# First two pairs of heads rearranged, and odd heads' score tiles in other units

## Chip, cores and metric

One core of one Trainium2 chip. The metric is device microseconds of a whole execution, as the median of several runs. TensorE does matmuls and transpositions, VectorE, ScalarE and GpSimd (POOL) work on tiles, SyncE (SP) issues most transfers; ScalarE can issue transfers too.

## What is computed

Attention that keeps only keys close to the row's largest score, then two feed-forward blocks. All in float32, results to float32 accuracy.

```python
# q, k, v: (4, 8, 576, 64); tau = 0.02
scores = q @ k.T / sqrt(64)
keep   = scores >= max(scores, -1) - tau
attn   = where(keep, exp(scores - max), 0);  attn /= sum(attn) + 1e-9
x      = (attn @ v) as rows of 2304 tokens x 512
h      = x @ w_in                       # 512 x 2048
x      = where(h >= 1, h, where(h <= -1, 0, (h + 1)**2 / 4)) @ w_out
h      = x @ w_in2                      # 512 x 1024
s      = h * softmax(h);  x = layernorm(s) * g_ln
out    = x @ w_out2
```

## The kernel before

Each float32 factor is held as a high part in the matmul's own format and a low part, the rounding rest, so a product of two factors takes several matmuls. For scores, the high and low parts of k and of q are stacked along the contraction: `k_st` and `q_st` hold 128 rows, `k_on` and `q_m` up to 67, of which three serve the row shifts. The stacking moves data between partitions and is done by transfers.

There are 32 heads in 16 pairs. A head has 5 score tiles of 128 queries by 576 keys. **Score tiles** (`sc`, `scores`) are only needed for the row maxima (`mcol`, `row_max`, VectorE). `row_shift` turns a head's five maxima into shifts (two ScalarE steps, three POOL steps), `shift_turn` transposes them on TensorE, `shift_store` copies them on ScalarE and sends them into `q_m` from ScalarE's queue. After that the **shifted tiles** (`zt`, `shifted`) are computed transposed, with the keys on partitions; `expo` (ScalarE) and `mask` (VectorE) follow, `p_split` makes `phi` (ScalarE) and `plo` (POOL), and three units later `values` does the `av` matmuls.

The unit of the attention loop is one shifted tile. A pair p has the nine units 9p to 9p+8: four tiles of the even head, one tile for the leftovers of both heads (unit 4 of the pair, with eight matmuls in place of four), four of the odd head. Units before 0 only prepare; the loop starts at `U0`. `ORDER` has a string per unit of a pair that says in which order the pieces of a unit are issued: E shifted tile and exp, S a score tile, x a maximum, M mask, v and V value matmuls, p the split, F the split of q and k (`split_kq`: high part `q_st` on ScalarE, low part `lo` on VectorE), P transpositions on TensorE, T transfers and other late things, A ScalarE steps, J one step of the weight jobs. `S_UNITS` says, relative to unit 9p, in which unit each of the ten score tiles of pair p is computed: five of the even head, five of the odd. `T_A` and `T_B` do the same for the transpositions of q and k (`tr`), `at` files a piece under its unit.

`tr`, `sc` and `zt` take turns in three PSUM slots (`ps_r`, three buffers in rotation): an allocation waits for the readers of the one that stood three before it. For `tr` the last reader is VectorE's `lo`, for `sc` the maximum, for `zt` the mask.

The weight jobs decode the first block's first weights, one 128 x 512 piece in many steps on ScalarE, VectorE and POOL. `DECODE` says which kinds of step may run in which unit of a pair (a: arrival, s and b: two kinds of VectorE steps), `JOBS_FROM` from which unit on, a new piece starts every 14 steps.

Each engine runs its instructions in the order written. SP's queue holds the loads of q and k (`load_kq`), of v (`load_v`), of weights and the stacking transfers of `stack_k` and `stack_q`.

Of the kernel before, what the change touches and what calls it, by code (L numbers as in the profile page):

```python
# [21 lines left out]
def kernel(  # L22
# [152 lines left out]
    def setup_fill(first):  # L175

        for i in range(max(NBUF)):
            for j in range(2):
                if i >= NBUF[j] or (i == 0) != first:
                    continue  # L180
# [1 line left out]
                nc.gpsimd.memset(f32(k_st[j][i][:, pad]), 0.0)
                nc.gpsimd.memset(f32(k_on[j][i][:, pad]), 0.0)
                nc.gpsimd.memset(f32(k_on[j][i][D:R3, 64 * j : 64 * j + S]), 1.0)
                nc.gpsimd.memset(f32(k_on[j][i][D:R1, 64 * j : 64 * j + S]), 0.0)
                nc.gpsimd.memset(f32(q_st[j][i][:, S:SP]), 0.0)
                nc.gpsimd.memset(f32(q_m[j][i][0:D, S:SP]), 0.0)
                nc.gpsimd.memset(f32(q_m[j][i][D:R3, :]), 0.0)
        for t in v_nat if first else ():
# [22 lines left out]
    def load_kq(p):  # L212
        t = early_p.tile([P, 2, NM + 1, 2, D], F32, tag="nat", name="nat", bufs=2)
        r0 = 2 * p * S
        two = q_rows[r0 : r0 + 2 * S, :].rearrange("(j s) d -> j s d", j=2)
        for j in range(2):
            nc.sync.dma_start(
                t[:, j, 0:NM, 1, :], two[j, 0:M4, :].rearrange("(p t) d -> p t d", t=NM)
            )
        nc.sync.dma_start(t[0:64, :, NM, 1, :], two[:, M4:S, :].rearrange("j s d -> s j d"))  # L220
# [2 lines left out]
        nc.sync.dma_start(t[:, 0, 0:NM, 0, :], k0)
        nc.sync.dma_start(t[64:P, 1, 0:NM, 0, :], k1[0:64])
        nc.sync.dma_start(t[0:64, 1, 1 : NM + 1, 0, :], k1[64:P])
        for j in range(2):
            nc.sync.dma_start(t[0:64, j, NM * (1 - j), 0, :], k_rows[r0 + M4 + 64 * j : r0 + M4 + 64 * j + 64, :])
        for j in range(2):
            nat_t[2 * p + j] = t[:, j]

    def load_v(p):
# [42 lines left out]
    def stack_k(h):  # L274
        j, i = buf(h)
        kh = f32(q_st[j][i][0:D, 0:S])
        o = slice(key_off(h), key_off(h) + S)
        if h < FAST:
            nc.scalar.copy(k_on[j][i][0:D, o], kh)
            nc.scalar.copy(q_m[j][i][0:D, 0:S], f32(q_st[j][i][D:P, 0:S]))  # L280
            nc.sync.dma_start(f32(k_st[j][i][0:D, o]), f32(k_on[j][i][0:D, o]))
        else:
            nc.sync.dma_start(f32(k_both[j][i][0:D, :, o]), kh.unsqueeze(1).to_broadcast([D, 2, S]))
# [843 lines left out]
```

## Time and profile before

| | us |
|---|---|
| median of 3 runs (984.61 to 988.9) | 985.89 |
| the profiled execution | 985.73 |
| its span, first to last instruction | 983.9 |
| TensorE busy | 953.3 (97%) |
| VectorE, ScalarE, POOL busy | 711.5, 494.6, 603.0 |
| first score tile starts | 18.28 |
| first shifted tile starts | 29.60 |
| first matmul of the feed-forward blocks | 375.89 |

A busy TensorE is not one at its peak: matmuls overlap in the pipeline, and at the lower clock they are busy for longer. Windows give the busy time of each engine in a stretch, with the number of its instructions; the timeline merges instructions of a kind that follow each other, and its bracket tells how long the engine idled before and what ended that; a wait of weight loads (PEld) for something is one of the matmul behind it.

### The profile page before, as it was taken

To read this page: it belongs to the slowest core of one execution; us is meant where nothing else is said; L and a number is where in the kernel's file an instruction comes from. 1 tells how busy PE (TensorE), PEld (TensorE's weight loads), DVE (VectorE), ACT (ScalarE), POOL (GpSimd) and SP (SyncE) were. 2 spreads that over 40 slices of the span, in tenths; PEclk is the share of its full clock that TensorE was granted. 3 is DMA by queue.
4 is the path that set the end of the run, shared out by engine and by line. 5 is a ranking of instruction groups with operands and counts; after the bars stand their busy time and mean duration, and the time that the engine had idled before them with its cause. 6 is when DMAs were issued, how large, how long until landed. Compare 5 with 4: busy or idle time off the path is not lost.

```text
span 983.9 us, 15050 instructions
## 1 busy us (share of the span) xinstructions
PE 953.3 (97%) x5232; PEld 839.6 (85%) x5232; DVE 711.5 (72%) x1128; ACT 494.6 (50%) x926; POOL 603.0 (61%) x573
## 2 busy tenths in 40 slices
PE   4999999999999999999999999999999999999998
PEld 3899988998899988889988998899889988888886
DVE  2788788878778755788767886788775686666561
ACT  2576776776676676454333333333334434434433
POOL 6477877987898788668545643564457704433422
PEclk9999999999999999999999999999999999999999
DMA  6565566666655513221221222111301214434453
GB/s 159 123 138 142 122 134 168 143 164 157 150 137 125 126 50 73 64 77 65 76 74 54 65 65 75 65 65 65 118 31 48 61 43 122 136 108 128 109 143 92
DMA packets 89885, 99.89 MB, mean 102 GB/s; under 512 B 50032, under 2 KB 62640, under 8 KB 89808
## 3 DMA queue, kind: packets, MB, share of 16 engines
...
q10 hardware_dynamic: 384, 0.16, 0.1%
...
## 4 chain that ended last, share of the span: by engine, by line
PE 77%; DVE 7%; ACT 5%; issue 3%; POOL 2%; SPq 2%; DMA 2%; ACTq 1%; DVEq 0%; POOLq 0%
PE y L801 20%; PE h L763 19%; PE o L956 10%; PE h L845 10%; PE av L430 7%; PE zt L380 6%; PE sc L303 4%; DVE e L398 3%; ACT e L393 2%; DVE mcol L316 2%; ACT phi L406 1%; DVE lo L269 1%; PE tr L260 1%; ACT xs L442 1%; DVE raw L501 1%
## 5 line engine op out<-in xcount | busy, mean ns | idle before, releaser
L407 POOL TENSOR_TENSOR plo<-e,phi 128x576 fp32r<-128x576 f32 x144 | 206.6, 1444 | 54.2 <-ACT phi L406 53.7
L784 POOL TENSOR_TENSOR gl<-cl,gh 128x512 fp32r<-128x512 f32 (+1 forms) x80 | 100.4, 1255 | 167.9 <-ACT gh L783 91.7
L801 PE MATMUL y<-gh,wg 128*128 128x512 f32 (+1 forms) x640 | 186.8, 373 | 0.0
L763 PE MATMUL h<-xh,wg 128*128 128x512 f32 (+1 forms) x640 | 184.2, 369 | 0.7 <-DVE e L398 0.7
L398 DVE SCALAR_TENSOR_TENSOR e<-zt,ntau,e 128x576 f32<-128x576 f32 x144 | 117.0, 813 | 63.5 <-ACT e L393 47.3
L801 PEld LDWEIGHTS y<-gh,wg 128*128 128x128 f32 x640 | 118.8, 188 | 17.1
L763 PEld LDWEIGHTS h<-xh,wg 128*128 128x128 f32 x640 | 118.4, 188 | 17.4 <-DVE e L398 1.0
L393 ACT ACTIVATE e<-zt 128x576 f32<-128x576 f32 x144 | 93.6, 650 | 74.7 <-PE zt L380 52.1
L801 PE MATMUL y<-gl,wg 128*128 128x512 f32 (+1 forms) x320 | 120.1, 375 | 0.5 <-POOL gl L784 0.4
L316 DVE TENSOR_REDUCE mcol<-sc 128x1 f32<-128x576 f32 x160 | 117.2, 748 | 3.8 <-PE sc L303 3.6
L763 PE MATMUL h<-xl,wg 128*128 128x512 f32 (+1 forms) x320 | 118.0, 369 | 0.0
L780 ACT ACTIVATE cl<-cl,half 128x512 f32<-128x512 f32 (+1 forms) x80 | 54.4, 680 | 98.5 <-DVE cl L779 98.4
L783 ACT CAST gh<-cl 128x512 fp32r<-128x512 f32 (+1 forms) x80 | 46.3, 578 | 112.5 <-DVE cl L782 106.7
L956 PE MATMUL o<-wg,ln 128*128 128x512 f32 x432 | 102.4, 393 | 0.0
L845 PE MATMUL h<-wg,y 128*128 128x512 f32 x432 | 101.2, 390 | 0.0
L406 ACT CAST phi<-e 128x576 fp32r<-128x576 f32 x144 | 96.3, 669 | 1.5 <-DVE e L398 0.9
L956 PEld LDWEIGHTS o<-wg,ln 128*128 128x128 f32 x432 | 80.9, 188 | 18.4 <-ACT ln L919 0.2
L845 PEld LDWEIGHTS h<-wg,y 128*128 128x128 f32 x432 | 81.0, 188 | 16.8
L920 POOL TENSOR_TENSOR ln<-land,ln 128x1024 fp32r<-128x1024 f32 x16 | 38.5, 2405 | 92.4 <-ACT ln L919 92.4
L779 DVE TENSOR_SCALAR cl<-h 128x512 f32<-128x512 f32 (+1 forms) x80 | 50.6, 632 | 55.1 <-PE h L763 51.3
L380 PE MATMUL zt<-q_st,k_both 128*128 128x288 f32 x320 | 75.1, 316 | 5.1 <-DVE lo L269 3.8
L303 PE MATMUL sc<-k_both,q_st 128*128 128x288 f32 x320 | 72.7, 310 | 5.4 <-DMA q_st<-lo 3.9
...
## 6 DMA issues: line engine op xcount, KB each, us to landing
...
```

The lines of the kernel that those rows point to most:

```text
L303: nc.tensor.matmul(ps[:, c, 0:HS], lhsT=st[j][i][r, n * P : n * P + P], rhs=kk[j][i][r, o + c * HS : o + (c + 1) * HS], start=(st is q_st) ...
L316: nc.vector.tensor_reduce(mc[:, n : n + 1], sc_ps.pop((h, n))[:, :, 0:HS], axis=AXES.XY, op=ALU.max, negate=True)
L380: nc.tensor.matmul(ps[:, c, 0:HS], lhsT=st, rhs=mv[:, c * HS : (c + 1) * HS], start=(m == 0), stop=(m == len(todo) - 1),)
L393: nc.scalar.activation(out=e, in_=st_ps[u][:, :, 0:HS], func=ACTF.Exp)
L398: nc.vector.scalar_tensor_tensor(out=e, in0=st_ps.pop(u)[:, :, 0:HS], scalar=ntau[:, 0:1], in1=e, op0=ALU.is_ge, op1=ALU.mult)
L406: nc.scalar.copy(hi, e)
L407: (nc.vector if u - NU in LO_DVE or u < NU - UNITS and u % UNITS in LO_UNITS else nc.gpsimd).tensor_tensor(lo, e, f32(hi), op=ALU.subtract)
L763: nc.tensor.matmul(ps, lhsT=a[:, kk, f], rhs=m[:, kk, :], start=(n == 0 and kk == 0), stop=(n == 2 and kk == KD - 1),)
L784: nc.gpsimd.tensor_tensor(gl, cl, f32(gh), op=ALU.subtract)
L801: nc.tensor.matmul(y_ps[c][d], lhsT=a[:, jj, ds_], rhs=m, start=(jj == 0 and n == 0), stop=(jj == JG - 1 and n == 2),)
L845: nc.tensor.matmul(ps[g], lhsT=a[:, kk, :], rhs=wg_t["in2", g][s][:, kk, :], start=(n < 2), stop=(n >= 6 * KD - 2),)
L956: nc.tensor.matmul(ps, lhsT=a[:, f, :], rhs=wg_t["out2", f // 4][m][:, f % 4, :], start=(n == 0), stop=(n == len(terms) - 1))
```

## The change

The first two pairs get a schedule of their own, and from the third pair on the odd heads' score tiles stand in units 4, 4, 5, 6, 7 of the pair before in place of 4, 5, 6, 6, 7. The preparation starts at unit -10 instead of -18. Loads of the first two pairs are split over SP's and ScalarE's queues, in another order; the first weight job, the values and the third pair's loads are issued later; stacking of heads 0 and 1 (`split_first`) uses copies on ScalarE, VectorE and POOL and two transfers a head. The fills of the padding are split up, and `keep_warm` adds transpositions of the identity matrix on TensorE, whose result nobody reads. `DECODE` lets no b step run in unit 8, and the weight jobs start at unit 1.

```diff
-    U0 = -18
+    U0 = -10
-    S_UNITS = (-10, -9, -7, -7, -6, -5, -4, -3, -3, -2)
+    S_UNITS = (-10, -9, -7, -7, -6, -5, -5, -4, -3, -2)
+    S_FIRST = ((-8, -7, -6, -5, -4, -3, -2, -1, -1, 0), (-8, -8, -7, -6, -6, -5, -4, -3, -3, -2))
+    WARM = (16, 14, 10)
+    KEEP = {-8: 1, -7: 1, -6: 1, -5: 1, -4: 1, -3: 4, -1: 6, 0: 4, 1: 4, 2: 4}
...
-        "EvvvSSSMxxxVLFPATpJ",
+        "EvvSvSSMxxxVLFPATpJ",
...
-        "FEvvvSSSMxxxVLPvATpJ",
+        "FEvvSvSSMxxxVLPvATpJ",
...
-    JOBS_FROM = -1
+    JOBS_FROM = 1
-    DECODE = ('', '', 's', 'asb', '', 's', '', 'as', 'asb')
+    DECODE = ('', '', 's', 'asb', '', 's', '', 'as', 'as')
...
+        for n, (dst, src) in enumerate(todo):
+            (nc.scalar if n in others else nc.sync).dma_start(dst, src)
...
+    def split_first():
+
+        srcs = [tr_t[h] for h in range(2)]
+        for h in range(2):
+            split_kq(h)
+            j, i = buf(h)
+            o = slice(key_off(h), key_off(h) + S)
+            nc.scalar.copy(k_st[j][i][0:D, o], f32(q_st[j][i][0:D, 0:S]))
+            nc.vector.tensor_copy(k_on[j][i][0:D, o], srcs[h][0:D])
+            nc.sync.dma_start(f32(k_st[j][i][D:P, o]), f32(tr_t[h][0:D, :]))
+            stack_q(h)
+            nc.gpsimd.tensor_copy(q_m[j][i][0:D, 0:S], f32(q_st[j][i][D:P, 0:S]))
+
+    def keep_warm(n):
+
+        ps = ps_av.tile([P, 2, 512], F32, tag="av", name="av")
+        for _ in range(n):
+            nc.tensor.transpose(ps[:, 0, 0:P], ident, ident)
...
+    load_kq(0, (1, 3, 5, 7))
+    load_kq(1, (1, 3, 5))
     nc.scalar.activation(out=warm, in_=one, func=ACTF.Exp)
-    load_kq(0)
...
-    jobs.step()
-    load_kq(1)
-    load_v(0)
-    setup_fill(True)
-    at(late_, T_FIRST[1] + 1, setup_fill, False)
+    setup_fill(0, nc.gpsimd)
+    setup_fill_v()
+    keep_warm(WARM[0])
+    at(pe_, U0, keep_warm, WARM[1])
+    at(pe_, U0 + 1, keep_warm, WARM[2])
+    at(first_, U0 + 1, split_first)
+    at(late_, U0 + 1, setup_ones)
+    at(late_, U0 + 1, setup_fill, 1, nc.gpsimd)
+    at(late_, -6, load_v, 0, nc.scalar)
+    at(late_, -4, load_kq, 2)
+    at(late_, -1, load_v, 1)
+    at(late_, 0, setup_fill, 2, nc.gpsimd)
+    for u, n in KEEP.items():
+        at(late_, u, keep_warm, n)
```

SP, from the raw weights to the first stacking transfers, before (`_98` and `_103` are the buffers of head 0, `_101` and `_106` of head 1, `_99` and `_104` of head 2):

```order
L519 DMA raw<-in_moe_w_in_dram 128x1024
L217 DMA nat<-in_q_dram 128x4x64 x2
L220 DMA nat<-in_q_dram 64x2x64
L223 DMA nat<-in_k_dram 128x4x64
L224 DMA nat<-in_k_dram 64x4x64
L225 DMA nat<-in_k_dram 64x4x64
L227 DMA nat<-in_k_dram 64x64 x2
L237 DMA v_nat_113<-in_v_dram 128x2x256
L243 DMA v_nat_113<-in_v_dram 64x64 x2
L281 DMA k_both_98<-k_both_98 64x576
L284 DMA k_both_98<-lo 64x576
L291 DMA q_st_103<-lo 64x576
```

And with the change, from the second pair's first load on:

```order
L238 DMA nat<-in_q_dram 128x4x64
L238 DMA nat<-in_k_dram 128x4x64
L238 DMA nat<-in_q_dram 128x4x64
L238 DMA nat<-in_k_dram 64x4x64 x2
L304 DMA k_both_98<-lo 64x576
L293 DMA q_st_103<-lo 64x576
L304 DMA k_both_101<-lo 64x576
L293 DMA q_st_106<-lo 64x576
L287 DMA k_both_99<-q_st_104 64x2x576
L288 DMA k_both_99<-lo 64x576
L289 DMA q_m_109<-q_st_104 64x576
L293 DMA q_st_104<-lo 64x576
```

Weights and values are gone from ahead of the stacking transfers; what is left ahead are loads of q and k, some of which ScalarE issues.

TensorE around the first shifted tiles, from the turn of head 0's shifts on, before:

```order
L340 MATMUL tm<-ident,mr 10x128
L303 MATMUL sc<-k_both_101,q_st_106 128x288 x2
L303 MATMUL sc<-k_both_101,q_m_111 128x288 x2
L260 MATMUL tr<-ident,nat 128x128 x4
L260 MATMUL tr<-ident,nat 128x64
L303 MATMUL sc<-k_both_99,q_st_104 128x288 x2
L303 MATMUL sc<-k_both_99,q_m_109 128x288 x2
L380 MATMUL zt<-q_st_103,k_both_98 128x288 x2
L380 MATMUL zt<-q_m_108,k_both_98 128x288 x2
```

And with the change, from the same turn on:

```order
L361 MATMUL tm<-ident,mr 10x128
L324 MATMUL sc<-k_both_101,q_st_106 128x288 x2
L324 MATMUL sc<-k_both_101,q_m_111 128x288 x2
L324 MATMUL sc<-k_both_101,q_st_106 128x288 x2
L324 MATMUL sc<-k_both_101,q_m_111 128x288 x2
L312 MATMUL av<-ident 128x128 x6
L401 MATMUL zt<-q_st_103,k_both_98 128x288 x2
L401 MATMUL zt<-q_m_108,k_both_98 128x288 x2
L324 MATMUL sc<-k_both_101,q_st_106 128x288 x2
L324 MATMUL sc<-k_both_101,q_m_111 128x288 x2
L312 MATMUL av<-ident 128x128 x4
```

The first shifted tile stood behind the last tile of head 1 and the first of head 2; now it stands ahead of both, and transpositions of the identity (`av<-ident`) stand between.

VectorE in units 2 to 5 of pair 5, from the masks of units 1 and 2 to that of unit 5, before:

```order
L398 SCALAR_TENSOR_TENSOR e<-zt,ntau,e 128x576 x2
L316 TENSOR_REDUCE mcol<-sc 128x1 x2
L491 TENSOR_SCALAR dec_a<-dec_a 128x512
L269 SCALAR_TENSOR_TENSOR lo<-tr,scale_119,q_st_104 128x576
L316 TENSOR_REDUCE mcol<-sc 128x1
L398 SCALAR_TENSOR_TENSOR e<-zt,ntau,e 128x576
L494 TENSOR_SCALAR dec_a<-dec_a 128x512
L398 SCALAR_TENSOR_TENSOR e<-zt,ntau,e 128x576
L316 TENSOR_REDUCE mcol<-sc 128x1
L398 SCALAR_TENSOR_TENSOR e<-zt,ntau,e 128x576
```

And with the change:

```order
L419 SCALAR_TENSOR_TENSOR e<-zt,ntau,e 128x576 x2
L337 TENSOR_REDUCE mcol<-sc 128x1 x2
L278 SCALAR_TENSOR_TENSOR lo<-tr,scale_119,q_st_104 128x576
L337 TENSOR_REDUCE mcol<-sc 128x1
L419 SCALAR_TENSOR_TENSOR e<-zt,ntau,e 128x576
L518 SCALAR_TENSOR_TENSOR dec_a<-raw,dec_a 128x512
L419 SCALAR_TENSOR_TENSOR e<-zt,ntau,e 128x576
L337 TENSOR_REDUCE mcol<-sc 128x1 x2
L419 SCALAR_TENSOR_TENSOR e<-zt,ntau,e 128x576
```

A decode step no longer stands ahead of `lo`, another one stands ahead of the mask of unit 4, and the maximum of the second odd tile stands one mask earlier. On TensorE that score tile went from unit 5 to unit 4, and the third odd one from unit 6 to unit 5. Units 6 now hold one score tile where they held two.

## Rows read from the trace of the kernel before

**Rows 1.** Windows; columns: stretch, its length, busy us (instructions) by engine, clock, DMA share, GB/s.

```profile
0.00:18.28 18.28, 4.21 (x16) 2.71 (x16) 2.40 (x11) 7.00 (x10) 15.65 (x56) 1.00 0.63 144
18.28:26.85 8.57, 8.57 (x36) 8.57 (x36) 6.62 (x9) 0.51 (x2) 0.66 (x4) 1.00 0.77 183
29.60:38.09 8.49, 7.15 (x46) 5.83 (x45) 6.92 (x10) 5.80 (x13) 3.42 (x5) 1.00 0.55 127
38.09:50.69 12.60, 12.55 (x93) 11.88 (x91) 9.83 (x16) 9.25 (x20) 9.77 (x10) 1.00 0.54 118
```

**Rows 2.** Timeline, start to first score tile: start us, length, engine, line, operation [idle before].

```profile
0.73 1.28 ACT L638 ACT_TABLE_LOAD   x1 [0.73 <-PEq L1109]
...
6.08 1.08 PE L260 MATMUL tr<-ident,nat 128*128 128x128 f32 x4 [6.08 <-DMA nat<-in_k_dram]
...
7.88 0.74 ACT L268 ACTIVATE q_st<-tr,scale 128x576 fp32r<-128x576 f32 x1 [5.65 <-PE tr L260]
...
13.01 1.11 SPq L243 DMA_DIRECT2D v_nat<-in_v_dram  x2
...
15.46 0.59 SPq L291 DMA_DIRECT2D q_st<-lo  x1
...
18.28 0.82 PE L303 MATMUL sc<-k_both,q_st 128*128 128x288 f32 x2 [3.37 <-DMA q_st<-lo]
```

**Rows 3.** Timeline, head 0's shift up to the first shifted tile.

```profile
24.24 0.21 ACT L326 ACTIVATE sh<-mcol 128x5 f32<-128x5 f32 x1 [7.55 <-DVE mcol L316]
...
25.39 0.20 POOL L330 TENSOR_TENSOR mr<-sh,mr 128x5 fp32r<-128x5 f32 x1
...
26.97 0.27 PE L340 MATMUL tm<-ident,mr 128*10 128x128 f32 x1
...
27.57 1.22 ACTq L347 DMA_DIRECT2D q_m<-mt  x1
...
29.60 0.42 PE L380 MATMUL zt<-q_st,k_both 128*128 128x288 f32 x2
```

**Rows 4.** Timeline of TensorE, first shifted tiles of pair 1 and of pair 14.

```profile
50.69 0.43 PE L380 MATMUL zt<-q_st,k_both 128*128 128x288 f32 x2
...
338.34 0.43 PE L380 MATMUL zt<-q_st,k_both 128*128 128x288 f32 x2
```

**Rows 5.** Waits of weight loads, pairs 1 to 13: total us, times, longest.

```profile
PEld zt L380 <- DVE lo L269: 7.5, 16, 0.9
PEld zt L380 <- DVE e L398: 4.4, 17, 0.3
...
PEld av L430 <- POOL plo L407: 3.8, 10, 0.7
```

**Rows 6.** Timeline of pair 5 from unit 3's decode step to unit 5.

```profile
147.18 1.27 DVE L491 TENSOR_SCALAR dec_a<-dec_a 128x512 f32<-128x512 f32 x1
...
148.37 0.81 DVE L269 SCALAR_TENSOR_TENSOR lo<-tr,scale,q_st 128x576 fp32r<-128x576 f32 x1
...
149.23 0.53 PE L380 MATMUL zt<-q_st,k_both 128*128 128x288 f32 x2 [0.32 <-DVE lo L269]
...
151.74 0.43 PE L380 MATMUL zt<-q_st,k_both 128*128 128x288 f32 x2
```

**Rows 7.** Timeline of TensorE, unit 4 of pair 13, no decode step before it.

```profile
325.66 0.43 PE L380 MATMUL zt<-q_st,k_both 128*128 128x288 f32 x2
```

**Rows 8.** Page, costliest groups: operation, forms, count, busy us, mean ns, idle before.

```profile
L407 POOL TENSOR_TENSOR plo<-e,phi 128x576 fp32r<-128x576 f32 x144 | 206.6, 1444 | 54.2 <-ACT phi L406 53.7
...
L398 DVE SCALAR_TENSOR_TENSOR e<-zt,ntau,e 128x576 f32<-128x576 f32 x144 | 117.0, 813 | 63.5 <-ACT e L393 47.3
...
L393 ACT ACTIVATE e<-zt 128x576 f32<-128x576 f32 x144 | 93.6, 650 | 74.7 <-PE zt L380 52.1
...
L316 DVE TENSOR_REDUCE mcol<-sc 128x1 f32<-128x576 f32 x160 | 117.2, 748 | 3.8 <-PE sc L303 3.6
```

**Rows 9.** Groups of lines, VectorE, pairs 1 to 13: a decode step.

```profile
L497 DVE SCALAR_TENSOR_TENSOR dec_a<-raw,dec_a 128x512 uint32<-128x512 uint32 x8 | 9.7, 1212 | 0.0
```

More of the change, by code (lines that the diff above doesn't have):

```diff
@@ L85 @@
     LO_DVE = ()
-    T_FIRST = (-17, -17)
-    T_SECOND = (-13, -2)
-    JOBS_FROM = -1
+    T_FIRST = (-10, -10)
+    T_SECOND = (-9, -3)
+    SPLIT_SECOND = (-8, -2)
+    JOBS_FROM = 1
     X_EARLY = 6
@@ L173, in setup, with setup_fill, setup_fill_v, setup_ones @@
         nc.vector.tensor_tensor(ntau, tau_sb, ntau, op=ALU.min)
[L175 to L180, printed above, removed]
-                pad = slice(S, SP) if j == 0 else slice(0, 64)
[L182 to L189, printed above, removed]
+    def setup_fill(i, eng):
+        for j in range(2):
+            if i < NBUF[j]:
+                pad = slice(S, SP) if j == 0 else slice(0, 64)
+                eng.memset(f32(k_st[j][i][:, pad]), 0.0)
+                eng.memset(f32(k_on[j][i][:, pad]), 0.0)
+                eng.memset(f32(k_on[j][i][D:R3, 64 * j : 64 * j + S]), 1.0)
+                eng.memset(f32(k_on[j][i][D:R1, 64 * j : 64 * j + S]), 0.0)
+                eng.memset(f32(q_st[j][i][:, S:SP]), 0.0)
+                eng.memset(f32(q_m[j][i][0:D, S:SP]), 0.0)
+                eng.memset(f32(q_m[j][i][D:R3, :]), 0.0)
+    def setup_fill_v():
+        for t in v_nat:
             nc.gpsimd.memset(t[64:P, 8, :], 0.0)
             nc.gpsimd.memset(t[0:64, 9, :], 0.0)
-        for t in () if first else v_hi:
+    def setup_ones():
+        for t in v_hi:
             nc.gpsimd.memset(f32(t[:, 0:8, D:P]), 1.0)
@@ L210, in main_rows, with load_kq, load_v @@
         ]
-    def load_kq(p):
-        t = early_p.tile([P, 2, NM + 1, 2, D], F32, tag="nat", name="nat", bufs=2)
+    def load_kq(p, others=()):
+        t = nat_t[p] = early_p.tile([P, 2, NM + 1, 2, D], F32, tag="nat", name="nat", bufs=2)
         r0 = 2 * p * S
         two = q_rows[r0 : r0 + 2 * S, :].rearrange("(j s) d -> j s d", j=2)
[L216 to L220, printed above, removed]
         k0 = k_rows[r0 : r0 + M4, :].rearrange("(p t) d -> p t d", t=NM)
         k1 = k_rows[r0 + M4 + P : r0 + 2 * S, :].rearrange("(p t) d -> p t d", t=NM)
[L223 to L231, printed above, removed]
+        rest = [
+            (t[0:64, j, NM * (1 - j), 0, :], k_rows[r0 + M4 + 64 * j : r0 + M4 + 64 * j + 64, :]) for j in range(2)
+        ]
+        main = [(t[:, j, 0:NM, 1, :], two[j, 0:M4, :].rearrange("(p t) d -> p t d", t=NM)) for j in range(2)]
+        todo = [
+            main[0],
+            (t[0:64, :, NM, 1, :], two[:, M4:S, :].rearrange("j s d -> s j d")),
+            (t[:, 0, 0:NM, 0, :], k0),
+            rest[0],
+            main[1],
+            rest[1],
+            (t[64:P, 1, 0:NM, 0, :], k1[0:64]),
+            (t[0:64, 1, 1 : NM + 1, 0, :], k1[64:P]),
+        ]
+        for n, (dst, src) in enumerate(todo):
+            (nc.scalar if n in others else nc.sync).dma_start(dst, src)
+    def load_v(p, eng=nc.sync):
         t = v_nat[p % 2]
@@ L275, in stack_k @@
         j, i = buf(h)
-        kh = f32(q_st[j][i][0:D, 0:S])
         o = slice(key_off(h), key_off(h) + S)
[L278 to L283, printed above, removed]
+        kh = f32(q_st[j][i][0:D, 0:S]).unsqueeze(1).to_broadcast([D, 2, S])
+        nc.sync.dma_start(f32(k_both[j][i][0:D, :, o]), kh)
         nc.sync.dma_start(f32(k_st[j][i][D:P, o]), f32(tr_t[h][0:D, :]))
-        if h < FAST:
-            return
         nc.sync.dma_start(f32(q_m[j][i][0:D, 0:S]), f32(q_st[j][i][D:P, 0:S]))
```

40 lines of the change are left out of this document (22 added, 18 removed).

## The prediction

> **What bounds the kernel now.** I read the windows by stage first, then the timeline of the first 40 us, then the waits of TensorE in the attention units, then single pairs. From the first value tile on TensorE has no slack: 12.55 us busy of 12.60, from 38.09 on [rows 1]. The stages behind attention are not touched, so only two things can move the end: when the attention loop gets going, and how long a pair of heads takes in it.
>
> The start is no TensorE time. Until 18.28 TensorE works 4.21 us [rows 1]. Head 0 is transposed from 6.08 and its high part is split at 7.88, but the transfer that stacks the low part of q leaves SP only at 15.46, behind the raw weights, the second pair and the value loads, whose last two go out at 13.01; the first score tile waits for it until 18.28 [rows 2]. Then 36 matmuls take 8.57 us without a gap, 0.238 us each, against 12.55/93 = 0.135 us later [rows 1]. For 288 columns the first is the 1.2 GHz level and the second the 2.4 GHz one; the clock column prints 1.00 in both stretches, so the durations have to tell the level. The first shifted tile (zt) of unit 0 starts at 29.60 [rows 3].
>
> The steady loop: unit 0 of pair 1 starts at 50.69, of pair 14 at 338.34 [rows 4], so 287.65/13 = 22.13 us a pair. Its 140 matmuls of 0.135 are 18.9 us, ten transpositions some 1.1; the other 2.1 us are refills of the pipeline and waits. Three waits show over these 13 pairs [rows 5]: zt for a PSUM slot that VectorE's lo still reads (7.5 us), zt for a mask (4.4), value matmuls for POOL's plo (3.8).
>
> **Part 1, the start.** SP now issues ten transfers before the first stacking one, none of them weights or values. Two issues took 1.11 us [rows 2], so at 0.56 to 0.65 each SP is free at about 7 and stacking waits for data alone. ScalarE pays: seven issues at 0.65, then the 1.28 us table load that used to begin at 0.73 [rows 2], leave it free at about 6.8, which is when head 0's transposition ends, its last large load being issued 1.3 us earlier. If an issue costs ScalarE what its own row shows, 1.22 us [rows 3], it is free at 10.8. I take 6.8, since SP's run of issues is nearer to a run of seven; the other end is +4.
>
> From 6.8: high part 0.74 [rows 2], low part 0.81 [rows 6], then the low parts of k and q are issued at 8.5 and 9.1. From issue to use it was 2.82 us [rows 2], so the first score tile has its data at 11.9 instead of 18.28. The copies to k_on and q_m, on VectorE and POOL, run beside that transfer. POOL's copy of 64x576 is in no row; its nearest is a subtraction of that length at 1.44 us [rows 8], so it costs between nothing and that and stays under the 2.8 us.
>
> TensorE must first pass 55 transpositions (16, 10, 14, 5, 10). Four took 1.08 us, the last seen whole [rows 2]: about 0.22 each at the low level, 12.1 us from 1.4 on, done at 13.5. If the clock rises among them they are done by 11.5. I take 12.5 for the first tile. The Trainium skill (TensorE: Matmul & The Clock Gate, Part 1) says that the low level is the default and that activity releases it; no run here shows yet whether transposing an identity counts. By that rule the first tile would start near 11.9 and part 1 be some 0.6 us better.
>
> A tile costs 0.54 us of TensorE and 0.75 of VectorE [rows 8], so VectorE sets the pace: five maxima from 13.3 to 17.2. The shift's steps on ScalarE and POOL took 24.24 to 25.59, its turn and copy 26.97 to 27.57; between them the turn stood behind queued tiles [rows 3]. Without that: 17.2 + 1.35 + 0.6 = 19.1. POOL must have its fills done; it had 15.65 us of work before 18.28 [rows 1], of which one set and a split now come later, so it is about in time. From issue to zt it was 2.03 us [rows 3], so zt of unit 0 starts at 21.2: -8.4 us.
>
> Half of that is given back. Units 0 to 3 hold six score tiles; it was four. I follow VectorE from the start of zt 0, with the durations of [rows 8]: maximum of head 1's last tile done at 2.0, mask 0 at 2.8; two tiles of pair 1, the first of which waits for mask 0's slot, at 5.1; mask 1 at 5.9. zt 2 waited for that slot, so exp and mask 2 end at 8.2. One maximum, lo, two maxima and mask 3, with 0.4 us of waiting for tiles, end at 12.4. Unit 4 starts at 12.5; it was 8.49 [rows 1]. The keep-warm transpositions, 12 x 0.11 = 1.3 us, lie inside these waits; without that cover they would cost those 1.3 us. Part 1: -8.4 + 4.0 = **-4.4 us**, bounds -6 and -0.4.
>
> The Trainium skill (Trainium Kernel Development and Optimization, Key Constraints) speaks against splitting the loads over SP and ScalarE: all transfers share the same 16 DMA engines, and a second issuer saves issue time only. Here issue time is what held stacking back, as [rows 2] show; if the bytes were the limit instead, the earlier transposition would go and part 1 be -3.7.
>
> **Part 2, the loop.** Odd tiles move from units 4, 5, 6, 6, 7 to 4, 4, 5, 6, 7. PSUM slots rotate in threes, so an allocation takes the slot that stood three before it.
> - Unit 7: zt followed two score tiles, so it took the slot of unit 6's zt and waited for its mask. Now it takes the score slot of unit 5, long read. The wait, 4.4/13 = 0.34 us a pair, goes: -4.6 over 13 pairs.
> - Unit 4: with a decode step of 1.27 us ahead of it, lo ends at 149.18 and zt starts at 149.23 after a wait [rows 6]; in a pair without one zt has no wait [rows 7]. Before, 9 of 13 pairs have a step there, now 2, because the jobs start later and one decode kind no longer runs in unit 8. Of the 7.5 us [rows 5] nine pairs carry most, 0.8 each, of which I count half as lo's own lateness that stays: 7 x 0.45 = -3.2.
> - Unit 5 gets a new wait: with two score tiles in unit 4 its zt takes the slot of unit 4's zt, so it waits for mask 4. From lo's end VectorE does a maximum, a mask, a decode step of up to 1.21 [rows 9] and a mask: 0.75 + 0.81 + 1.21 + 0.81 = 3.58. TensorE, if zt 4 starts right at lo's end, takes the old 2.51 [rows 6] plus 0.54 = 3.05. So the wait is 0.5 if lo is late and 0 if lo was half a microsecond early; behind it on TensorE stands all of unit 5. I take 0.3 with its refill: +3.9, bounds 0 and +8.
> - Tiles in units 2 and 7 now stand ahead of the plo matmuls, which gives POOL 0.54 us more: of the 3.8 us some -1.5.
>
> Part 2: **-5.4 us**, bounds -12 and +1. The last weight job now ends behind the last mask, one VectorE step and three others, needed only by the fourth output block: between 0 and +1, I take 0.3.
>
> Sum: -4.4 - 5.4 + 0.3 = -9.5 on the profiled execution of 985.73 (span 983.9 and 1.8 around it), which stands 0.16 under the median of the runs; from 985.9 that is 976.4, and as part 1's pieces lean to the early side I say **976.0 us**.
>
> **Rivals.**
> - The clock rises late: transpositions do not count, and the first tiles run at 0.238 us a matmul as before. First tile near 14, zt 0 near 25; units 0 to 3 are VectorE's anyway. Part 1 is -0.5: 980.3. For it: the transpositions of the old start left the level low; against: they were 4.21 us of work in 18.28 [rows 1]. Chance 0.18.
> - The loop gains nothing: unit 5 waits 0.5 us in every pair, 2.6 more than forecast, and decode steps delay lo elsewhere for as much again. Part 2 is 0: 981.8. For it: VectorE is busy 9.83 of 12.60 [rows 1] and in order. 0.17.
> - The loop gains more: unit 5 does not wait and lo is always early. Part 2 is -11: 970.8. 0.12.
> - Slower: the clock stays low through the thin first units, where TensorE waits for VectorE. Then all up to unit 4 is TensorE's at twice its time: zt 0 at 28, units 0 to 3 take 16.8 (8.4 us of matmuls at the high level), unit 4 starts at 45, and of 8.57 us more of unbroken work before the rise [rows 1] half is lost: 49.3 against 38.1, +11.2, so 992.0. It decides when the level is still low at zt 0, and the kernel is slower as soon as that costs more than part 2 gives, 5.1. For it: waits of 1 to 2 us in the plan above; against: 1.34 us of idling in 8.49 did not drop the old kernel [rows 1]. 0.07.
>
> **How the numbers follow.** The forecast has 0.46, with 972 to 980 as its own range. About 0.5%, 4.9 us, is what a measurement of this kernel can tell from no change, so faster ends at 981.0. Faster: 0.46 + 0.12 + 0.12 of the 0.18 + 0.06 of the 0.17 = 0.76. Within: 0.06 + 0.11 + 0.02 of the slow case = 0.19. Slower: 0.05. The range of 968 to 983 leaves out the slow case and the best one's tail.
>
> **What would show it.** Right: the first score tile at 11.5 to 13 with 0.135 us a matmul; zt 0 near 21; unit 4 near 34; no wait of zt for a mask in unit 7, a new one under 0.6 us in unit 5; pairs of about 21.7. Wrong: ScalarE issuing until after 9, score tiles at 0.24 us a matmul, or a unit 5 that waits 0.8.

## The result, and the profile after

The changed kernel takes 976.34 us (median; 973.72 to 977.29) against 985.25 for the old one beside it: ratio 0.9901, 95% interval [0.9875, 0.9927]. Repeated later it took 976.24 (973.15 to 980.93). The forecast was 976.0. The total came out, but not by the terms that were summed, and the rest of this text is about those.

The profiled execution took 977.29 us, its span is 975.5. Three stages, in us, taken from the starts of shifted tiles (unit 0 of pairs 1 and 14) and of the first feed-forward product:

| | before | after | difference | forecast |
|---|---|---|---|---|
| start to unit 0 of pair 1 | 50.69 | 45.00 | -5.69 | -4.4 |
| pairs 1 to 13 | 287.65 | 282.57 | -5.08 | -5.4 |
| pair 14 to the first product | 37.55 | 39.47 | +1.92 | +0.3 |
| the rest of the span | 608.0 | 608.5 | +0.5 | 0 |

Line numbers of the changed kernel are others than before: zt L401, sc L324, mask L419, maximum L337, tr L269, lo L278, plo L428, identity L312.

Windows of the changed kernel, from the start to the first score tile, to the first shifted tile, to unit 4, to pair 1 (columns as in [rows 1]; the engines are TensorE, its weight loads, VectorE, ScalarE, POOL):

```profile
0.00:12.09 12.09, 9.34 (x56) 7.87 (x56) 3.62 (x13) 4.84 (x7) 8.78 (x36) 1.00 0.61 133
12.09:20.37 8.28, 7.77 (x57) 7.11 (x58) 7.27 (x11) 1.57 (x5) 5.09 (x17) 1.00 0.73 171
20.37:32.44 12.07, 9.82 (x67) 8.32 (x66) 7.43 (x11) 6.02 (x12) 8.02 (x14) 1.00 0.68 166
32.44:45.00 12.56, 12.51 (x92) 11.81 (x91) 8.66 (x13) 8.58 (x19) 8.53 (x10) 1.00 0.55 135
```

Timeline of its start, answering to [rows 2, 3] (start, length, then what ended the idle time):

```profile
1.35 3.67 PE L312 MATMUL av<-ident 128*128 128x128 f32 x16 [1.35 <-POOL ident masks.py:199]
...
5.93 1.28 ACT L661 ACT_TABLE_LOAD   x1 [5.93 <-DMA nat<-in_q_dram]
...
7.33 0.72 ACT L277 ACTIVATE q_st<-tr,scale 128x576 fp32r<-128x576 f32 x1
8.09 1.75 PE L312 MATMUL av<-ident 128*128 128x128 f32 x14
...
9.56 0.54 SPq L293 DMA_DIRECT2D q_st<-lo  x1
...
12.09 0.50 PE L324 MATMUL sc<-k_both,q_st 128*128 128x288 f32 x2 [0.36 <-DMA q_st<-lo]
...
18.66 1.42 ACTq L368 DMA_DIRECT2D q_m<-mt  x1
...
20.37 0.51 PE L401 MATMUL zt<-q_st,k_both 128*128 128x288 f32 x2
21.41 0.53 PE L401 MATMUL zt<-q_m,k_both 67*128 67x288 f32 x2 [0.53 <-DMA q_m<-mt]
```

The transfer that stacks q leaves SP at 9.56 instead of 15.46, and the first score tile starts at 12.09 instead of 18.28. The second row of the windows holds the maxima and the shift, 8.28 us against 11.32 before. Units 0 to 3, the third row, take 12.07 against 8.49: the part given back. Sixteen identity transpositions take 3.67 us, fourteen later ones 1.75: 0.23 and 0.125 us each on average, so the clock rose between them.

Waits of weight loads in pairs 1 to 13 (total us, times, longest), answering to [rows 5]:

```profile
PEld sc L324 <- DVE e L419: 4.2, 7, 1.0
...
PEld sc L324 <- DVE dec_a L518: 3.0, 2, 1.5
PEld tr L269 <- DVE e L419: 2.1, 11, 0.6
PEld zt L401 <- DVE lo L278: 1.3, 2, 0.9
PEld av L451 <- POOL plo L428: 1.0, 5, 0.2
PEld zt L401 <- DVE e L419: 0.8, 5, 0.2
```

The three waits of [rows 5] fell from 15.7 to 3.1 us. In their place score tiles wait 7.2 us, where before only 1.3 us were put down to them. 4.7 us of this stand at the first odd tile in unit 4 of pairs 2, 7, 11 and 12. The two longest, in pairs 7 and 11, are put down to a decode step of VectorE. It ended 0.2 and 0.3 us before the tiles started, and e4_q_early below shows that they don't wait for it. Pair 7, on TensorE:

```profile
182.71 0.43 PE L401 MATMUL zt<-q_st,k_both 128*128 128x288 f32 x2
...
185.28 0.50 PE L324 MATMUL sc<-k_both,q_st 128*128 128x288 f32 x2 [1.34 <-DVE dec_a L518]
```

And on SP, the same stretch:

```profile
174.12 1.19 SPq L490 DMA_DIRECT2D rb<-rec  x2
175.40 0.53 SPq L540 DMA_DIRECT2D raw<-in_moe_w_out_dram  x1
176.04 0.64 SPq L287 DMA_DIRECT2D k_both<-q_st  x1
...
180.39 0.22 SPq L465 DMA_DIRECT2D sums<-xs  x1
180.66 0.46 SPq L466 DMA_DIRECT2D x<-xs  x1
182.88 0.46 SPq L293 DMA_DIRECT2D q_st<-lo  x1
```

q of the odd head is stacked over the rows that `k_both<-q_st` reads, so its transfer may only leave when that one has landed, and it stands behind the stores of sums and x. SP's own waits (45 to 348 us):

```profile
SPq L293 <- DMA k_both<-q_st: 14.9, 10, 2.7
```

In pair 7 the reciprocals and a raw weight block are ahead of k's stacking, which leaves at 176.04; q leaves 6.8 us later, at 182.88, 1.8 us behind the end of the stores, and the tile starts 2.4 us after that. In a quiet pair q leaves 7.05 us after unit 0 begins and the tile is due at 9.6 (1.06 us after unit 4's shifted tile starts): 2.5 us, with nothing to spare. In pairs 2 and 12 q leaves on time and takes 3.2 and 3.5 us.

In pair 11 the same wait is followed by a slower stretch (windows of units 4 and 5):

```profile
269.08:272.65 3.57, 2.34 (x16) 1.92 (x15) 3.17 (x5) 2.68 (x7) 2.54 (x3) 1.00 0.60 150
272.65:276.07 3.42, 3.42 (x17) 3.37 (x16) 1.46 (x2) 0.53 (x2) 2.78 (x5) 0.50 0.87 195
```

From 272.65 to 276.07 the granted clock is 0.50, the 1.2 GHz level; seventeen matmuls take 3.42 us where 0.135 us each would be 2.3. TensorE had idled 1.23 us up to 271.79. Pair 7's idle time of 1.34 us was followed by no such stretch: the granted clock is 1.00 from 185.28 to 192.00. Pair 11 takes 24.18 us, pair 13 21.26.

### The profile page after: what moved, and what is told of

The parts are those of the page before. It is cut to its first block, busy times and chain, and to the rows that moved or that the text cites. A ratio compares the mean times of both kernels' runs of the same rounds, so it can differ in the third digit from the quotient of the medians.

```text
span 975.5 us, 15180 instructions
## 1 busy us (share of the span) xinstructions
PE 954.8 (98%) x5299; PEld 845.2 (87%) x5299; DVE 714.8 (73%) x1130; ACT 495.5 (51%) x924; POOL 603.3 (62%) x575
## 4 chain that ended last, share of the span: by engine, by line
PE 87%; POOL 4%; DVE 3%; issue 2%; ACT 2%; DMA 1%; ACTq 0%; DVEq 0%; POOLq 0%; SPq 0%
PE y L828 20%; PE h L790 20%; PE av L451 10%; PE o L983 10%; PE h L872 10%; PE zt L401 7%; PE sc L324 7%; POOL plo L428 2%; PE tr L269 2%; DVE e L419 1%; DMA nat<-in_q_dram 1%; ACT e L414 0%; ACT phi L427 0%; POOL wg L558 0%; POOL x L498 0%
## 5 line engine op out<-in xcount | busy, mean ns | idle before, releaser
L428 POOL TENSOR_TENSOR plo<-e,phi 128x576 fp32r<-128x576 f32 x144 | 207.3, 1449 | 55.5 <-ACT phi L427 55.4
L419 DVE SCALAR_TENSOR_TENSOR e<-zt,ntau,e 128x576 f32<-128x576 f32 x144 | 116.6, 812 | 54.9 <-ACT e L414 37.3
L337 DVE TENSOR_REDUCE mcol<-sc 128x1 f32<-128x576 f32 x160 | 116.8, 748 | 6.9 <-PE sc L324 6.7
L872 PEld LDWEIGHTS h<-wg,y 128*128 128x128 f32 x432 | 81.0, 188 | 16.8
L324 PE MATMUL sc<-k_both,q_st 128*128 128x288 f32 x320 | 71.1, 304 | 6.7 <-DVE dec_a L518 2.6
L401 PE MATMUL zt<-q_st,k_both 128*128 128x288 f32 x320 | 72.9, 309 | 0.9 <-DVE lo L278 0.9
```

The lines of the kernel that those rows point to most:

```text
L324: nc.tensor.matmul(ps[:, c, 0:HS], lhsT=st[j][i][r, n * P : n * P + P], rhs=kk[j][i][r, o + c * HS : o + (c + 1) * HS], start=(st is q_st) ...
L337: nc.vector.tensor_reduce(mc[:, n : n + 1], sc_ps.pop((h, n))[:, :, 0:HS], axis=AXES.XY, op=ALU.max, negate=True)
L401: nc.tensor.matmul(ps[:, c, 0:HS], lhsT=st, rhs=mv[:, c * HS : (c + 1) * HS], start=(m == 0), stop=(m == len(todo) - 1),)
L419: nc.vector.scalar_tensor_tensor(out=e, in0=st_ps.pop(u)[:, :, 0:HS], scalar=ntau[:, 0:1], in1=e, op0=ALU.is_ge, op1=ALU.mult)
L428: (nc.vector if u - NU in LO_DVE or u < NU - UNITS and u % UNITS in LO_UNITS else nc.gpsimd).tensor_tensor(lo, e, f32(hi), op=ALU.subtract)
L872: nc.tensor.matmul(ps[g], lhsT=a[:, kk, :], rhs=wg_t["in2", g][s][:, kk, :], start=(n < 2), stop=(n >= 6 * KD - 2),)
```

## The experiments

All are the changed kernel with the edit shown. Stages in us are those of one profiled execution, whose time stands behind them; it can be the slowest of its kernel's 4 to 6 runs, so stages must not be added up to the median. The ratio is to the old kernel on the same chip:

| run | to pair 1 | pairs 1-13 | pair 14 to product | this execution | median | ratio, 95% |
|---|---|---|---|---|---|---|
| changed kernel | 45.00 | 282.57 | 39.47 | 977.29 | 976.34 | 0.9901 [0.9875, 0.9927] |
| a2_again | 45.89 | 285.32 | 39.42 | 980.93 | 976.24 | 0.9902 [0.9877, 0.9927] |
| e1_no_warm | 49.81 | 280.05 | 39.41 | 979.56 | 977.21 | 0.9923 [0.9903, 0.9943] |
| e6_no_keep | 49.41 | 279.75 | 39.43 | 979.57 | 976.69 | 0.9914 [0.9897, 0.9931] |
| e5_one_queue | 48.00 | 281.06 | 39.42 | 978.58 | 977.73 | 0.9922 [0.9904, 0.994] |
| e2_old_units | 45.44 | 281.32 | 39.44 | 976.29 | 978.63 | 0.9933 [0.9912, 0.9954] |
| e3_old_decode | 45.93 | 283.55 | 37.19 | 976.85 | 978.21 | 0.9925 [0.9904, 0.9946] |
| e4_q_early | 45.79 | 277.90 | 39.42 | 972.98 | 973.02 | 0.9873 [0.9852, 0.9894] |
| f2_tail | 44.61 | 279.30 | 38.79 | 972.44 | 973.69 | 0.9882 [0.9865, 0.9899] |
| f1_all | 44.93 | 278.22 | 39.97 | 972.77 | 973.08 | 0.9876 [0.9861, 0.9892] |
| f5_pool | 45.84 | 287.79 | 37.19 | 980.80 | 977.13 | 0.9912 [0.989, 0.9934] |
| f3_best | 45.81 | 280.95 | 37.75 | 974.57 | 974.08 | 0.9874 [0.9854, 0.9895] |
| f4_both_q | 44.87 | 280.13 | 37.67 | 972.62 | 972.45 | 0.9859 [0.9836, 0.9882] |

Differences of 2 us between medians are near what the intervals can tell, so stages and waits carry most verdicts, though each is of one execution.

**a2_again: are the waits the kernel's own?** No edit.

> The changed kernel once more, on the chip of these runs. If the late q of pairs 2, 7, 11, 12 and 14 and the clock's fall in pair 11 belong to the kernel, they stand in the same pairs again: 975.5 to 977.5. If they are an accident of one execution, unit 4 waits in other pairs, or the fall is elsewhere or absent; the time is within 973.5 to 977.5 either way.

The waits of pairs 2, 7, 11 and 14 stand there again, with 0.71, 2.27, 2.77 and 0.68 us beyond the tile's due time (0.70, 1.50, 1.63 and 0.67 in the first run); that of pair 12 doesn't. Pair 14's is nothing new: it was 0.73 in the old kernel. Here pair 7's is put down to the transfer itself (TensorE), and a slow stretch follows it, and another follows pair 11's:

```profile
187.04 0.50 PE L324 MATMUL sc<-k_both,q_st 128*128 128x288 f32 x2 [2.11 <-DMA q_st<-lo]
```

Windows of the three stretches at clock 0.50:

```profile
27.67:31.09 3.42, 3.42 (x16) 2.95 (x16) 1.84 (x3) 2.11 (x4) 0.97 (x1) 0.50 0.76 182
...
188.10:191.51 3.41, 3.41 (x16) 3.36 (x16) 1.17 (x2) 0.58 (x2) 1.71 (x4) 0.50 0.92 212
...
276.85:280.26 3.41, 3.41 (x17) 3.38 (x16) 1.52 (x2) 0.00 (x0) 1.64 (x4) 0.50 0.84 190
```

The place is the kernel's and the length of the wait varies from run to run. The clock falls behind three of these four long waits, and not behind pair 7's of the first run. The first row is a fall behind unit 2 of pair 0, in the thin start, which the first run didn't have. Profiled executions of e2_old_units, e4_q_early, f3_best and f5_pool have it too, between 27 and 32 us; those of e3_old_decode and e5_one_queue have one between 7.5 and 13.5 us.

**e4_q_early: q of the odd head ahead of the stores.**

```diff
-                at(late_, t + (STACK[1] - 1 if p > 1 else 1), stack_q, h)
+                at(late_, t + (STACK[1] - 1 - j if p > 1 else 1), stack_q, h)
```

> The changed kernel with the stacking transfer of an odd head's q issued one unit earlier, ahead of the stores of sums and x. Theory, the first odd score tile of unit 4 waits for that transfer because SP is held behind those stores: the waits of 0.7 to 1.6 us in pairs 2, 7, 11, 12 and 14 go, and the drop of the clock that followed the longest of them in pair 11 as well: 970.5 to 973.5. Rival, the transfer is late by its data (the split) or by the queues of the DMA engines: the waits stay and the kernel at 975.5 to 977. Second rival, the stores behind it become late and hold ScalarE's or POOL's buffers: 977 to 980.

973.02, in the range. In pair 2 q now leaves 3.6 us after unit 0 begins, ahead of the stores (SP):

```profile
71.26 0.46 SPq L293 DMA_DIRECT2D q_st<-lo  x1
73.90 0.24 SPq L465 DMA_DIRECT2D sums<-xs  x1
```

The waits of pairs 2, 12 and 14 are gone; pairs 7 and 11 still wait 0.62 and 1.04. Their transfers are late by the reader of the overwritten rows: in pairs 7 and 11 q leaves 6.1 and 5.9 us after k's stacking, which stands behind `rb` and `raw`, and in pair 2 only 3.4. That is now SP's longest wait (from 160 to 300 us):

```profile
SPq L293 <- DMA k_both<-q_st: 14.0, 9, 3.2
```

In pair 11 the tile starts while the decode step that the first run's wait was put down to still runs (VectorE, 268.83 to 270.19), so it doesn't wait for that step:

```profile
269.90 0.50 PE L324 MATMUL sc<-k_both,q_st 128*128 128x288 f32 x2 [0.88 <-DMA q_st<-lo]
```

The clock doesn't fall in pairs 1 to 15. The four runs also lie closer together, 972.1 to 973.4, where the changed kernel's ten lie between 973.15 and 980.93; that points to the late q as the source of most of its spread.

**e2_old_units: the old units of odd tiles.**

```diff
-    S_UNITS = (-10, -9, -7, -7, -6, -5, -5, -4, -3, -2)
+    S_UNITS = (-10, -9, -7, -7, -6, -5, -4, -3, -3, -2)
```

> The changed kernel with the old units of odd heads' score tiles (4, 5, 6, 6, 7) in the loop, all else new. Theory, the new units end the wait of unit 7's zt for a mask: the wait comes back, 0.3 to 0.4 us a pair, unit 5's short wait for mask 4 goes, pairs 22.0 instead of 21.74, 978.5 to 981. Rival, the gain of the loop came from lo and the decode steps alone: pairs stay at 21.74 and the kernel at 976 to 977. Second rival, two tiles in unit 4 mostly meet a late transfer of q, so that the old units are better: 973 to 975.

978.63. The wait for a mask is back, 15 times in pairs 1 to 13 (waits of weight loads):

```profile
PEld zt L401 <- DVE e L419: 4.2, 15, 0.5
```

The first theory holds for the wait, not for the pairs' length: 281.32/13 = 21.64 is no longer than 21.74, because this profiled execution had no fall of the clock in pairs 1 to 13 and shorter waits for q. Pairs without either (6, 8, 10) take 21.22, 21.14 and 21.20 here and 20.99, 20.97 and 20.98 in the changed kernel: the new units are worth 0.21 us a pair, 2.7 over 13, not the 0.34 that the wait alone would give. The waits for q stand in both, so the new units aren't their cause.

**e3_old_decode: the old places of decode steps.**

```diff
-    JOBS_FROM = 1
+    JOBS_FROM = -1
-    DECODE = ('', '', 's', 'asb', '', 's', '', 'as', 'as')
+    DECODE = ('', '', 's', 'asb', '', 's', '', 'as', 'asb')
```

> The changed kernel with the weight jobs' old start and old places for decode steps, new units of tiles. Theory, steps ahead of lo cost some 0.4 us in each of 7 pairs, and jobs that reach into the last pairs cost 2 us: unit 4's zt waits 0.3 to 1 us in 9 pairs or more, the last pair gets back 2 us, the sum is 976 to 978. Rival, lo has become early enough to hide a step: only the tail's 2 us come back, 973.5 to 975. Second rival, the tail's loss isn't the jobs': 979 to 980.

978.21, just above the first theory's sum. The wait for lo is back, longer than in [rows 5] (waits of weight loads):

```profile
PEld zt L401 <- DVE lo L278: 9.4, 17, 0.9
```

So steps ahead of lo cost 8.1 us of waits (9.4 against 1.3), and the last two pairs get 2.3 us back, as the theory has it. But pairs 1 to 13 are only 1.0 us longer (283.55 against 282.57), which the theory doesn't have. With lo late, unit 4 begins 8.9 to 9.7 us after unit 0 instead of 8.5 to 9.5, while q leaves at 7.0 to 7.6: the waits of unit 4's first odd tile fall from 4.75 to 0.4 us, and no slow stretch follows one. In pairs 7 and 11 raw loads also stand elsewhere. The wait for lo covers the one for q.

**e1_no_warm: no identity transpositions.** All 67 go (the expectation says 30 for the 27 of `KEEP`).

```diff
-    WARM = (16, 14, 10)
-    KEEP = {-8: 1, -7: 1, -6: 1, -5: 1, -4: 1, -3: 4, -1: 6, 0: 4, 1: 4, 2: 4}
+    WARM = (0, 0, 0)
+    KEEP = {}
...
+        if n == 0:
+            return
```

> The changed kernel without its 40 + 30 identity transpositions (nothing of the result is left out). Theory, they raise the clock: the level stays low at the first score tiles, 0.238 us a matmul instead of 0.135, TensorE paces units 0 to 3, unit 4 of pair 0 starts at 36 to 42 instead of 32.44, and the kernel takes 979.5 to 986. Rival, VectorE and the transfers pace the start whatever the clock: unit 4 starts at 32 to 33.5, 975.5 to 977. Second rival, they only fill the queue ahead of the first tile: it starts earlier than 12.09 and the kernel is 975 or less.

The first tile starts at 12.09 as with them, but at the low level, and the level stays low into unit 4 (TensorE; L402 is zt here, L325 sc):

```profile
12.09 0.82 PE L325 MATMUL sc<-k_both,q_st 128*128 128x288 f32 x2 [1.38 <-DMA q_st<-lo]
...
36.79 0.68 PE L402 MATMUL zt<-q_st,k_both 128*128 128x288 f32 x2
...
38.00 0.43 PE L402 MATMUL zt<-q_m,k_both 67*128 67x288 f32 x2
```

Pair 1 starts 4.8 us later than in the changed kernel, unit 4 at 36.79 as the first theory has it. This execution, the slowest of its five, takes 979.56 us, 2.3 more than the changed kernel's: its loop lost less to the late q, though the clock fell once in its pair 3. The median, 977.21, is only 0.9 higher, below that theory's range. That the identity transpositions raise the clock is shown; that it pays 4.8 us in the end is not, since the loop's waits move with the start.

**e6_no_keep: the warm-up stays, the 27 later ones go.**

```diff
-    KEEP = {-8: 1, -7: 1, -6: 1, -5: 1, -4: 1, -3: 4, -1: 6, 0: 4, 1: 4, 2: 4}
+    KEEP = {}
```

> The changed kernel without the 27 identity transpositions of units -8 to 2, the 40 of the warm-up left in (nothing of the result is left out). Theory, they keep the clock up through the thin units: without them the granted clock falls between 12 and 32 us, units 0 to 3 take 13.5 to 17 us instead of 12.07, 977.5 to 981. Rival, waits of a microsecond or two there don't drop it: units 0 to 3 as before or 0.3 to 1 us shorter, 975 to 976.5.

The clock falls in the thin units (windows from unit 0 on):

```profile
21.69:23.76 2.07, 0.77 (x6) 0.54 (x5) 1.08 (x2) 0.72 (x1) 0.80 (x1) 1.00 0.37 79
23.76:37.42 13.66, 13.56 (x55) 12.17 (x54) 8.26 (x11) 5.61 (x11) 7.72 (x14) 0.50 0.62 156
```

It stays at 0.50 for 13.66 us, units 0 to 3 take 14.7 us instead of 12.07, pair 1 starts 4.4 us later: the first theory in the trace. The median, 976.69, lies between the two theories' ranges; the profiled execution (979.57) is again the slowest of five, and again its loop lost less to the late q.

**e5_one_queue: all loads of q and k from SP.**

```diff
-    load_kq(0, (1, 3, 5, 7))
-    load_kq(1, (1, 3, 5))
+    load_kq(0)
+    load_kq(1)
```

> The changed kernel with all 16 loads of the first two pairs issued by SP, none by ScalarE. Theory, issue time is what the split over two engines saves: SP issues seven transfers more at 0.55 to 0.65 us before the first stacking one, which goes out at 11.5 to 13 instead of 9.56, the first score tile comes 2 to 3 us later than 12.09, and the kernel takes 977.5 to 979.5. Rival, the bytes or the splits on ScalarE are the limit: ScalarE is free earlier, the first tile at 11.5 to 12.5, 975 to 976.5.

ScalarE's first split starts earlier, at 6.70 instead of 7.33, but stacking waits for SP, which issues loads until 11.73 (timeline):

```profile
12.49 0.54 SPq L293 DMA_DIRECT2D q_st<-lo  x1
...
15.24 0.50 PE L324 MATMUL sc<-k_both,q_st 128*128 128x288 f32 x2 [0.93 <-DMA q_st<-lo]
```

The first tile comes 3.15 us later and pair 1 3.0 us; the median is 977.73. Issue time is what the two queues save, as the first theory has it.

**f2_tail: decode steps elsewhere, done by pair 14.**

```diff
-    DECODE = ('', '', 's', 'asb', '', 's', '', 'as', 'as')
+    DECODE = ('', '', '', 'asb', '', 'sb', '', 'asb', 'a')
```

> The changed kernel with another table of places for decode steps: two places a pair for the steps on two operands instead of one, and none ahead of lo; the last step is then in pair 14. Theory, steps of the weight jobs in the last pair cost 2 us: pair 14 to the first product behind attention takes 37 to 38 us instead of 39.47, and steps ahead of lo in two pairs and in unit 0 a little more, 973 to 974.5. Rival, the last pair is late for another reason: 39.5 stays, 975.5 to 977. Second rival, steps ahead of masks 6 and 8 cost what they save: 975 to 977.

973.69, in the first theory's range, but the last two pairs get back only 0.7 us. The kernel gains by the loop; f5_pool settles what holds the end.

**f5_pool: decode steps done by pair 13.**

```diff
-    DECODE = ('', '', 's', 'asb', '', 's', '', 'as', 'as')
+    DECODE = ('', 'sb', '', 'asb', '', 'sb', '', 'asb', 'a')
```

> The changed kernel with another table of places for decode steps alone: four places a pair, none ahead of lo, all steps by pair 13. Theory, after f2_tail: what holds the last pair is POOL, on which an addition and a subtraction of the last weight job (2.6 us) stand between the low parts of values' weights in pairs 14 and 15; with both earlier, pair 14 to the first product behind attention takes 37.1 to 37.7 us as before the change, not 38.8 to 39.5, and the kernel 972.5 to 974. Rival, the last pair is late by its tiles or by ScalarE: 38.8 or more, 973.5 to 975.

The end is as the theory says: 37.19 us, as in e3_old_decode. In the changed kernel two job steps stand among POOL's plo (timeline of the changed kernel, pairs 14 and 15):

```profile
337.87 1.31 POOL L529 TENSOR_TENSOR dec_a<-dec_a,raw 128x512 f32<-128x512 f32 x1 [0.63 <-DVE raw L525]
339.15 1.42 POOL L428 TENSOR_TENSOR plo<-e,phi 128x576 fp32r<-128x576 f32 x1
...
348.33 1.29 POOL L558 TENSOR_TENSOR wg<-dec_a,wg 128x512 fp32r<-128x512 f32 x1
349.58 1.41 POOL L428 TENSOR_TENSOR plo<-e,phi 128x576 fp32r<-128x576 f32 x1
```

From pair 14 on its value matmuls wait 3.3 us for plo; in f5_pool (waits of the same stretch):

```profile
PEld av L451 <- POOL plo L428: 0.2, 1, 0.2
```

But the total is missed, 977.13 against 972.5 to 974: the new step in unit 1 stands ahead of mask 2, and the transpositions of unit 2, which take that tile's turn in the three PSUM slots, wait for it (waits in pairs 1 to 13):

```profile
PEld tr L269 <- DVE e L419: 12.8, 13, 1.4
```

That is 2.1 us in the changed kernel. The place had looked free, as VectorE has no maxima there.

**f1_all: the edits of e4_q_early and f2_tail, and loads moved.**

```diff
-    JOB_EVERY = 14
+    JOB_EVERY = 12
-    NORM = (13, 6, 4)
+    NORM = (14, 5, 4)
-        def step(self, kinds="asb", many=1):
+        def step(self, kinds="asb", many=1, start=True):
...
-            if self.todo and self.now >= self.next and len(self.live) < self.depth:
+            if start and self.todo and self.now >= self.next and len(self.live) < self.depth:
-                jobs.step("asb" if u < 0 else DECODE[u % UNITS])
+                jobs.step("asb" if u < 0 else DECODE[u % UNITS], start=u % UNITS in (1, 2, 3, 4, 5))
```

> The changed kernel with three edits: an odd head's stacking of q one unit earlier, the decode steps of the run f2_tail, and the loads of raw weights and of reciprocals kept out of the units ahead of unit 0, where they stood before k's stacking in pairs 7 and 11. Theory, each takes away its own wait: no score tile of unit 4 waits over 0.3 us, 37 to 38 us from pair 14 on, pairs of 21.2, 969 to 971.5. Rival, of the steps on one chain only one counts: 972 to 973.5, as the earlier stacking alone.

973.08, the rival's range. Unit 4's tiles wait 0.13 us at most, and in pair 7 q leaves 3.4 us after k's stacking instead of 6.8. The reciprocals still stand ahead of k's stacking there, the raw block doesn't, which points to the raw block as what held it. So far the theory holds; but in pairs 1, 10 and 11 the tile ahead of unit 8 waits 0.8 to 1.1 us, in pair 10 for the even head's q (stacked at 15.8 us after unit 0 instead of 14.4), and the end stays long.

**f3_best and f4_both_q: f1_all with `DECODE` of f5_pool and raw loads behind units 5 and 6; the last edit, the even head's q, is f4_both_q's alone.**

```diff
-    JOB_EVERY = 14
+    JOB_EVERY = 10
-                jobs.step("asb" if u < 0 else DECODE[u % UNITS])
+                jobs.step("asb" if u < 0 else DECODE[u % UNITS], start=u % UNITS in (5, 6))
...
-                at(late_, t + (STACK[1] - 1 - j if p > 1 else 1), stack_q, h)
+                at(late_, t + (STACK[1] - 2 if p > 1 else 1), stack_q, h)
```

> The changed kernel with an odd head's q stacked one unit earlier, raw weights loaded only behind units 5 and 6, reciprocals one unit later, and decode steps in four places a pair, none ahead of lo, all by pair 13. Theory, the three losses of the changed kernel (score tiles of unit 4 that wait for q, the raw load ahead of k's stacking, POOL's job steps in the last pair) are separate and all go: pairs of 21.1, 37.2 to 37.8 us from pair 14 on, 968 to 971. Rival, each wait that goes uncovers VectorE's masks in units 5 to 7: 971 to 973.5, as the runs e4_q_early and f1_all.

> The run f3_best with the even head's q stacked one unit earlier as well. Theory, the first even tile in unit 8 waits for it in 2 to 4 pairs, up to 1 us each: 0.5 to 2 us under f3_best. Rival, SP then stands waiting for k's transfer with the loads behind it: 0 to 2 us above f3_best.

974.08 and 972.45: f3_best lies above even its rival's range of 971 to 973.5, f4_both_q 1.6 under it, as its theory has it. In f3's profiled execution the clock falls twice, behind unit 2 of pair 0 and in pair 2. In f4's unit 4 loses some 0.3 us in all, the clock doesn't fall at all, and the end takes 37.67; but the transpositions wait 8.8 us (pairs 1 to 13), f5_pool's fault again:

```profile
PEld tr L269 <- DVE e L419: 8.8, 13, 1.4
```

f4_both_q is the fastest of all kernels here (972.16 to 972.66), 3.8 us under a2_again on the same chip; that it beats e4_q_early (0.6 us) is within the spread. A table of steps that ends by pair 13 and spares mask 2 wasn't run.

## Why the forecast held, step by step

The sum of part 2 (-5.4, measured -5.08) came out in good part by luck: three of its terms (unit 5, lo, plo) were too pessimistic by 8 us together, and losses that stood in no term took about as much. Part 1 gained 1.3 us more than was said, the end lost 1.6 more.

- **Start of stacking**: right. ScalarE's issues ended at 5.90, its table load at 7.21 (forecast 6.8), the first tile came at 12.09 (forecast 11.9 to 12.5), e5_one_queue shows that issue time was the limit. The Trainium skill (Trainium Kernel Development and Optimization, Key Constraints) says that a second issuer saves issue time only; e5_one_queue agrees, and that time was 3 us here.
- **Clock**: right in kind. The level rose before the first score tile, and e1_no_warm shows that the identity transpositions did it. The Trainium skill (TensorE: Matmul & The Clock Gate, Part 1) says that activity releases the clock; these runs agree for transpositions whose result nobody reads. The rival with the low level up to unit 4 was over-priced: it said 11.2 us, e1_no_warm and e6_no_keep have that state and start pair 1 4.8 and 4.4 us later. In e1_no_warm unit 0 starts at 23.25 where the rival had 28, units 0 to 3 take 13.54 us where it had 16.8, and the level rises 0.9 us into unit 4.
- **Shift and first shifted tile**: 20.37 against 21.2, though its second half waited until 21.41 for the shifts. Units 0 to 3 took 12.07 against 12.5. Both sizes are 0.4 to 0.8 off to the same side, so part 1 is -5.7 where -4.4 was said. In a2_again, with its fall of the clock in pair 0, it is -4.8.
- **Unit 7's wait** went (4.4 to 0.8 us for all waits of zt for masks). e2_old_units brings it back.
- **lo in unit 4**: 7.5 to 1.3, twice the -3.2 of the sum. Counting half of each wait as lo's own lateness was the error: where no step stands ahead, lo is early.
- **Unit 5's new wait**, +3.9 in the sum, is the term that failed most. It lies within the 0.8 us that zt waits for masks at all, none of these over 0.2. The bound of 0 was the right end: lo ends early, and two tiles in unit 4 give VectorE the time, though no run tests this by itself.
- **plo**: -2.8 for -1.5.
- **What stood in no term**: q of the odd head, due in unit 4, with 2.5 us from issue to use and nothing to spare. In pairs 2, 7, 11 and 12 it cost 0.70 + 1.50 + 1.63 + 0.92 = 4.75 us, and some 1.1 to 1.5 more by the clock behind pair 11's. Without these the loop would be near -11, the rival "the loop gains more", with 970.8; e4_q_early, which takes most of them away, comes to 973.02. This loss and lo's gain are not independent. The first odd tile stood in unit 4 before the change too; there the wait for lo ([rows 6]: zt at 149.23) let q land in time, 3.4 us from issue to use in pair 5 of the old kernel:

```profile
146.97 0.55 SPq L291 DMA_DIRECT2D q_st<-lo  x1
...
150.40 0.43 PE L303 MATMUL sc<-k_both,q_st 128*128 128x288 f32 x2
```

So the gain at lo uncovered the wait behind it; e3_old_decode, which makes lo late again, covers it again. It could have been seen in the old trace, but only TensorE's and VectorE's queues were followed for part 2.

- **End**: +1.9 for +0.3. The forecast counted one VectorE step behind the last mask; it was two POOL steps of 1.3 us among the plo of pairs 14 and 15, where POOL also splits values and scales x. e3_old_decode and f5_pool, which move them, both end in 37.19.

Open: the waits of [rows 5] and their successors add to less than the loop's 5.08 (-12.6 + 5.9 for score tiles + 1.5 for transpositions + 1.1 for the clock = -4.1). The rest may be refills behind fewer waits; no row shows it. Why the late q cost less in e1_no_warm and e6_no_keep, whose starts were later, is also open: in pair 7 of e1_no_warm k's stacking left 1.4 us after unit 0 instead of 2.0, but not why. And that an idle TensorE makes the clock fall rests on their standing together in several runs, with pair 7 of the changed kernel against it; no run set the length of the idle time by itself. Nor does any run show why the identity transpositions held the level in pair 0 of some executions and not of others.
